# Scores of 13 chunks laid across all partitions through a line of DRAM instead of a TensorE transpose, and gate's row spread one turn earlier

## The chip, the cores and the metric

The kernel runs on one core of one Trainium2 chip. The metric is device time in microseconds: 203.6 us before the change, the median of three runs (203.56 to 203.7). The profile is of one execution, with a span of 201.8 us from first to last instruction.

## The reference

Two blocks follow one another. The first is a linear attention with data-dependent decay (RWKV6): for each batch and head a state of 48 x 48 is carried over 768 time steps.

```python
for t in range(S):
    cur = np.einsum('bhd,bhe->bhde', u[None] * kt, vt)
    y[:, :, t] = np.einsum('bhd,bhde->bhe', rt, state + cur)
    state = wt[:, :, :, None] * state + np.einsum('bhd,bhe->bhde', kt, vt)
```

Here (batch, heads, steps, head size) is (4, 8, 768, 48). The result, as x of (4, 768, 384), goes into a mixture of depths: a row's score is its product with w_gate; in each batch the 128 rows with the highest scores pass through a two-layer network, are weighted and added back.

```python
scores = np.einsum('bsd,d->bs', x, w_gate)
top_idx = np.argpartition(-scores[b], capacity)[:capacity]
ye = np.maximum(x[b, top_idx] @ w1, 0.0) @ w2
out[b, top_idx] = x[b, top_idx] + sigmoid(scores[b, top_idx])[:, None] * ye
```

All is in float32. The last line is shortened here; the reference writes the sigmoid out.

## The kernel before

The 768 steps of a batch are cut into NCH = 6 chunks of L = 128, which makes 24 chunks over B = 4 batches, numbered through: chunks 0 to 5 are batch 0, chunks 6 to 11 batch 1, and so on. The function `turn(i)` writes the work of one turn, from -2 to 24. The order is written out by hand (`tc.manual_schedule`): each engine runs its instructions in exactly the order in which `turn` names them, and the framework only adds the waits. A turn mixes work on several chunks, called by `step(function, chunk)`:

- `scores` (L379) for chunk i: the products of K and R into ps_s; `masked` (L387) on VectorE makes sc from it; `back` (L272, L397) turns K round again; `outputs_t` (L412 with sc, L420 with the carried state) makes ps_yt, which ScalarE copies into yt (L425).
- for chunk i-1: `rows_out` turns yt into rows (ps_y, L272), ScalarE copies them (L436), GpSimd adds the own term (L437), and SyncE sends x to out (L438). `row_products` (L442, GpSimd) and `row_sums` (L447, ScalarE) make the chunk's 128 scores, a column of `score` with one value in each partition.
- for chunk i+1: `inputs_t` transposes r (L265, ps_t), and `scaled` (L343) makes R from it with the scan `left`; for K likewise with the scan `right`.
- for chunk i+2: `decays_t` transposes w (L265, ps_w), and `scans` (L285, L291, L293, L296) runs the two running products on VectorE.
- `loads(i+5)`: SyncE issues v, k, r and w some turns ahead; `load_weights` sends a piece of w1 or w2 in seven of the turns.

What the change touches is `compared`. To find a row's rank, each score of a batch must be compared with every other. One of two must then stand along the free dimension, equal in all partitions. For chunk i-2, TensorE transposes the score column, repeated to 128 x 128, into ps_e (L508); VectorE compares the chunk's own scores with those of the earlier chunks (L510, on `every`) and with its own chunk (L514, on ps_e); ScalarE copies ps_e into `every` for the chunks to come (L519). ps_e and ps_w share the pool psW, which has one buffer: ps_w must wait until ps_e has been read, and ps_e until the scans have read the last ps_w. `compared` stands ahead of `masked` in the turn.

After the last chunk of a batch, `mixture` counts the lost comparisons on TensorE (ps_r, L534), picks the 128 rows (L551, ps_i L558), gathers them by an indirect transfer (L573) and transposes them (L582). Their two layers (`forward`: ps_h L618, ps_f L630) are fed in pieces into the turns of the next batch; those of the last batch come at the end. `spread(wg_bc, wg_row)` puts the row of w_gate in all partitions with two matmuls (ps_b, L258) and a ScalarE copy (L259); it stands in turn 0, behind `back`. `warm` is a filler matmul on zeros (ps_n, L253).

Of the kernel before, what the change touches and what calls it, by code (L numbers as in the profile page):

```python
# [10 lines left out]
FP32 = mybir.dt.float32  # L11
# [7 lines left out]
L = 128  # L19
# [6 lines left out]
def _rows(ap, n):  # L26

    return dataclasses.replace(ap, ap=[[0, n]] + [list(x) for x in ap.ap])
# [10 lines left out]
def kernel(  # L39
# [40 lines left out]
    nc = tc.nc  # L80
    PSUM = bass.MemoryType.PSUM

    B, H, S, D = r.shape
# [3 lines left out]
    NCH = S // L  # L87
# [11 lines left out]
    setup = ctx.enter_context(tc.tile_pool(name="setup", bufs=1))  # L99
    lev = ctx.enter_context(tc.tile_pool(name="lev", bufs=2))  # L100
    mod = ctx.enter_context(tc.tile_pool(name="mod", bufs=1))
    psW = ctx.enter_context(tc.tile_pool(name="psW", bufs=1, space=PSUM))
    psT = ctx.enter_context(tc.tile_pool(name="psT", bufs=2, space=PSUM))
    psS = ctx.enter_context(tc.tile_pool(name="psS", bufs=1, space=PSUM))
# [4 lines left out]
    chunks = [(b, ci) for b in range(B) for ci in range(NCH)]  # L109
# [17 lines left out]
    for queue, hs in ((nc.sync, slice(H // 2, H)), (nc.scalar, slice(0, H // 2))):  # L127
        queue.dma_start(
            out=w_bufs[0][:, hs, 0:D], in_=w[0, hs, 0:L, :].rearrange("h t d -> t h d")
# [4 lines left out]
    wg_row = setup.tile([1, C], FP32)  # L134
    nc.scalar.dma_start(out=wg_row, in_=_rows(moe_w_gate, 1))
    u_bc = consts.tile([L, H, D], FP32)
    wg_bc = consts.tile([L, C], FP32)
# [46 lines left out]
    ident = consts.tile([L, L], FP32)  # L184
# [13 lines left out]
    for x in (0, 1):  # L198
        for to, src in ((0, DP * x), (D, DP * (1 - x)), (2 * D, D)):
            n = min(D, DE - to)  # L200
# [12 lines left out]
    for t, sign in ((before_f, 1), (after_f, -1)):  # L213
        nc.gpsimd.memset(t, 1.0)
        nc.gpsimd.affine_select(
            out=t, in_=t, pattern=[[sign, L]], base=-1, channel_multiplier=-sign,
# [28 lines left out]
    score = consts.tile([L, B, NCH], FP32)  # L245
# [3 lines left out]
    def warm(n):  # L249

        ps = psM.tile([L, 512], FP32, tag="m", name="ps_n")
        for _ in range(n):
            nc.tensor.matmul(ps, nothing[:, 0:L], nothing, start=True, stop=True)  # L253

    def spread(to, row):

        ps = psM.tile([L, C], FP32, tag="m", name="ps_b")
        nc.tensor.matmul(ps, one_row, row, start=True, stop=True)  # L258
        nc.scalar.copy(out=to, in_=ps)  # L259
# [229 lines left out]

    against = {}  # L490

    def compared(t):

        b, ci = chunks[t["n"]]
        if ci == 0:
            while len(against) > 1:
                mix()
            against[b] = (
                mod.tile([L, S - L], FP32, name="every", bufs=2),
                mod.tile([L, NCH, S], BF16, name="ahead", bufs=2),  # L500
                lost_bufs[b % 2],
            )
        every, ahead, lost = against[b]
        own = score[:, b, ci:ci + 1]
        lo, hi = ci * L, (ci + 1) * L

        ps = psW.tile([L, L], FP32, tag="w", name="ps_e")
        nc.tensor.transpose(ps, own.to_broadcast([L, L]), ident)  # L508
        if ci > 0:
            nc.vector.tensor_scalar(  # L510
                out=ahead[:, ci, 0:lo], in0=every[:, 0:lo], scalar1=own, scalar2=None,
                op0=ALU.is_ge, op1=ALU.add, accum_out=lost[:, ci, 0:1],
            )
        nc.vector.scalar_tensor_tensor(  # L514
            out=ahead[:, ci, lo:hi], in0=ps, scalar=own, in1=after_f,
            op0=ALU.is_ge, op1=ALU.mult, accum_out=lost[:, ci, 1:2],
        )
        if ci < NCH - 1:
            nc.scalar.copy(out=every[:, lo:hi], in_=ps)  # L519

    def mixture(b):
# [130 lines left out]
    def step(f, n, *more):  # L652
        if 0 <= n < N:
            f(work.setdefault(n, dict(n=n)), *more)

    def mix(n=1, place=None):


        while n > 0 and mixing:
            if place is not None and mixing[0][1] not in (None, place):  # L660
                return
            try:
                mixing[0][1] = next(mixing[0][0])
                n -= 1
            except StopIteration:
                mixing.pop(0)
# [16 lines left out]
    def fed_in_turn(n, few):  # L683

        kept = (feed or picked) and (feed or picked)[0][0] == B - 2
        fed(few if kept else n, on=False)
# [6 lines left out]
    def turn(i):  # L693
        soon = i >= N - 1
        step(first_left, i + 1)
        if i < 1:
            step(scaled_aside, i + 1, "K", "right")
        step(own_products, i + 1)
        step(scores, i)
        step(own_values, i)  # L700
        step(carry, i - 1, work.get(i))
        if i > 0:
            step(scaled, i + 1, "K", "right")
        if i >= 0:
            step(own_weights, i + 1)
        if soon:
            step(masked, i)
        if i == N - 1:
            sums.extend(check_sums())
        if i < N:  # L710
            step(compared, i - 2)
        if not soon:
            step(masked, i)
        step(back, i)
        if i == 0:
            spread(wg_bc, wg_row)
        mix(place="half")
        step(rows_out, i - 1, soon)
        step(row_scores_soon if soon else row_products, i - 1)
        step(own_results, i)  # L720
        fed_in_turn(PIECES // 2, 2 if i >= N - 1 else 1)
        step(inputs_t, i + 1, "R", r_bufs)
        if i == -1:
            warm(1)
        step(scaled, i + 1, "R", "left")
        step(decays_t, i + 2)
        mix(place="mid")
        if i == -2:
            warm(2)
        step(range_check, i + 2)  # L730
        if i == -1:
            spread(u_bc.rearrange("p h d -> p (h d)"), u_row)
            step(own_weights, i + 1)
        step(outputs_t, i)
        step(carry_products, i)
        fed_in_turn(PIECES - PIECES // 2, 1 if i == N - 1 else 0)
        if i == N - 1:
            step(compared, i - 1)
        step(inputs_t, i + 2, "K", k_bufs)
        if i == -2:  # L740
            warm(1)
        if not soon:
            step(row_sums, i - 1)
        step(scans, i + 2)
        if 0 <= i - 2 < N - 1 and chunks[i - 2][1] == NCH - 1:
            mixing.append([mixture(chunks[i - 2][0]), "end"])
        mix(place="end")
        if i > -2:
            loads(i + 5)
        if i in WEIGHT_TURNS:  # L750
            load_weights(1)
# [23 lines left out]
    def general(gen):  # L775
        u_t = gen.tile([D, H], FP32, name="u_t")
        nc.sync.dma_start(out=u_t, in_=u.rearrange("h d -> d h"))
        for b in range(B):
            st = gen.tile([D, H, D], FP32, name="st")
            nc.vector.memset(st, 0.0)  # L780
            with tc.For_i(0, S) as i:
                now = {}
                for name, x in (("r", r), ("k", k), ("w", w)):
                    now[name] = gen.tile([D, H], FP32, name=f"{name}_t")
                    src = x[b, :, bass.ds(i, 1), :].rearrange("h o d -> d (h o)")
                    nc.sync.dma_start(out=now[name], in_=src)
                v_t = gen.tile([D, H, D], FP32, name="v_t")
                src = v[b, :, bass.ds(i, 1), :].rearrange("h o d -> (h o) d")
                nc.sync.dma_start(out=v_t, in_=_rows(src, D))
                kv = gen.tile([D, H, D], FP32, name="kv")  # L790
                nc.vector.tensor_mul(kv, v_t, now["k"].to_broadcast([D, H, D]))
                cur = gen.tile([D, H, D], FP32, name="cur")
                nc.vector.tensor_mul(cur, kv, u_t.to_broadcast([D, H, D]))
                nc.vector.tensor_add(cur, cur, st)
                nc.vector.tensor_mul(cur, cur, now["r"].to_broadcast([D, H, D]))
                nc.vector.tensor_mul(st, st, now["w"].to_broadcast([D, H, D]))
                nc.vector.tensor_add(st, st, kv)
                ps = psM.tile([L, C], FP32, tag="m", name="ps_g")
                nc.tensor.matmul(
                    ps[0:1], ones_f[0:D], cur.rearrange("p h d -> p (h d)"),  # L800
                    start=True, stop=True,
                )
                y_t = gen.tile([1, C], FP32, name="y_t")
                nc.scalar.copy(out=y_t, in_=ps[0:1])
                nc.sync.dma_start(out=out[b, bass.ds(i, 1), :], in_=y_t)
            for c in range(NCH):
                x = lev.tile([L, C], FP32, tag="x", name="x", bufs=3)
                nc.sync.dma_start(out=x, in_=out[b, c * L:(c + 1) * L, :])
                t = dict(n=b * NCH + c, x=x)
                row_scores_soon(t)  # L810
                compared(t)
            for _ in mixture(b):
                pass
            fed(1000)

    with tc.If(outside > 0):
        with tc.tile_pool(name="gen", bufs=1) as gen:
            general(gen)
# [26 lines left out]
```

## Time and profile before

| What | Value |
|---|---|
| Time, median of 3 | 203.6 us |
| Span of the profile | 201.8 us |
| TensorE matmul busy | 189.9 us (94%) |
| VectorE busy | 161.2 us (80%) |
| GpSimd busy | 136.7 us (68%) |
| ScalarE busy | 121.0 us (60%) |
| ps_e transposes (L508) | 24, 7.6 us, 318 ns each |
| Compare with earlier chunks (L510) | 20, 12.1 us, 605 ns each |
| Compare with own chunk (L514) | 24, 8.4 us, 348 ns each |
| Copy of ps_e into every (L519) | 20, 5.3 us, 263 ns each |
| Packets of SyncE's queue | 104304, 75.1% of 16 DMA engines' span |

Busy time is a sum over an engine's records; on TensorE records overlap, since matmuls are pipelined. The chain of work that ended last is followed back from the last instruction: at each step to what released it, or to the instruction before it on its engine. In order of time it lists start, length and what; "issue" is time in which the profile shows no reason to wait. In the timeline a note in brackets gives the idle time before an instruction and what ended it. SPq is SyncE's queue: there an instruction's length is that of the issue[...]. The DMA engines are at least nine tenths busy in nearly all of the first 100 us.

### The profile page before, as it was taken

How to read it: one execution, taken by the hardware profiler on the slowest of the kernel's cores; microseconds unless marked ns; L12 is line 12 of the kernel's file. 1: busy time of each engine (PE TensorE's matmuls, PEld its weight loads, DVE VectorE, ACT ScalarE, POOL GpSimd, SP SyncE). 2: the span in 40 equal slices, each digit the busy share in tenths (PEclk: the TensorE clock that was granted, in tenths of full speed). 3: DMA queues.
4: the chain of work that ended last, by engine and by line, in shares of the span. 5: the costliest groups of instructions: out<-in, count | busy, mean ns of one | idle time of the engine just before them, and what ended most of it. 6: DMA issues, size and time to landing. Idle time of an engine off the chain costs nothing.

```text
span 201.8 us, 6402 instructions
## 1 busy us (share of the span) xinstructions
PE 189.9 (94%) x2290; PEld 153.6 (76%) x2290; DVE 161.2 (80%) x355; ACT 121.0 (60%) x620; POOL 136.7 (68%) x175
## 2 busy tenths in 40 slices
PE   7899999989799899999999999999999999999980
PEld 3478888768687688888887888898887888876940
DVE  6989999999999968988979788988979784961010
ACT  4486877768854775878354865878354866510300
POOL 8497889886857996678538898669538898111202
PEclk9999999999999999999999999999999999999998
DMA  7999999999999999999892994998772221111101
GB/s 115 164 163 153 175 191 206 247 205 216 203 158 255 234 172 217 225 236 180 146 157 59 176 189 105 147 165 151 125 117 68 49 81 44 39 42 42 39 8 44
DMA packets 105387, 28.81 MB, mean 143 GB/s; under 512 B 100482, under 2 KB 104580, under 8 KB 105348
## 3 DMA queue, kind: packets, MB, share of 16 engines
q1 hardware_dynamic: 104304, 26.65, 75.1%
q0 software_dynamic: 512, 1.57, 2.6%
q8 instruction: 20, 0.33, 0.7%
q14 instruction: 19, 0.16, 0.3%
q10 hardware_dynamic: 532, 0.10, 0.3%
HBM read 22.81 MB, written 5.51 MB: 140 GB/s over the span
## 4 chain that ended last, share of the span: by engine, by line
PE 86%; DVE 5%; ACT 2%; POOL 2%; issue 2%; POOLq 0%; DVEq 0%; ACTq 0%
PE ps_s L379 12%; PE ps_h L618 11%; PE ps_f L630 11%; PE ps_yt L412 11%; PE ps_t L265 9%; PE ps_w L265 6%; PE ps_yt L420 5%; PE ps_kv L467 5%; PE ps_y L272 4%; PE ps_t L272 4%; PE ps_e L508 3%; PE ps_n L253 1%; DVE left L296 1%; DVE right_buf L285 1%; PE ps_r L534 1%
## 5 line engine op out<-in xcount | busy, mean ns | idle before, releaser
L364 ACT ACTIVATE rk<-rk 128x48 f32<-128x48 f32 x192 | 43.7, 231 | 0.1
L364 ACT ACTIVATION_READ_ACCUMULATOR rk<-rk 128x1 f32 x192 | 36.3, 189 | 0.0
L437 POOL TENSOR_TENSOR x<-x,vo 128x384 f32<-128x384 f32 x22 | 22.1, 1005 | 19.9 <-ACT x L436 19.8
L425 ACT COPY yt<-ps_yt 128x512 f32<-128x512 f32 x24 | 14.1, 587 | 29.6 <-PE ps_yt L420 27.1
L296 DVE TENSOR_TENSOR_SCAN left<-ps_w,from_left 128x511 f32<-128x511 f32 x24 | 30.7, 1281 | 0.9
L285 DVE TENSOR_TENSOR_SCAN right_buf<-ps_w,from_right 128x511 f32<-128x511 f32 x24 | 29.1, 1211 | 1.1 <-PE ps_w L265 1.1
L387 DVE TENSOR_TENSOR sc<-ps_s,before_f 128x1024 f32<-128x1024 f32 x24 | 29.2, 1219 | 0.8 <-PE ps_s L379 0.8
L379 PE MATMUL ps_s<-R,K 48*128 48x128 f32 x384 | 27.9, 285 | 0.3 <-ACT yt L425 0.2
L412 PE MATMUL ps_yt<-sc,v_buf 128*64 128x128 f32 x384 | 26.3, 278 | 1.6 <-PE ps_w L265 1.4
L379 PEld LDWEIGHTS ps_s<-R,K 48*128 48x128 f32 x384 | 23.3, 187 | 3.9 <-issue 2.9
L618 PE MATMUL ps_h<-xeT,w 128*128 128x128 f32 x192 | 25.6, 280 | 0.2 <-ACT hid L623 0.2
L355 POOL TENSOR_TENSOR rk<-r_buf,k_buf 128x384 f32<-128x384 f32 x24 | 24.2, 1007 | 1.7 <-DMA r_buf<-in_r_dram 1.7
L412 PEld LDWEIGHTS ps_yt<-sc,v_buf 128*64 128x64 f32 x384 | 20.7, 136 | 6.0 <-PE ps_w L265 2.8
L358 POOL TENSOR_TENSOR rk<-rk,u_bc 128x384 f32<-128x384 f32 x24 | 24.1, 1003 | 1.1 <-DVE alls L291 0.5
L618 PEld LDWEIGHTS ps_h<-xeT,w 128*128 128x128 f32 x192 | 22.9, 192 | 1.6 <-ACT xeT L584 0.5
L630 PE MATMUL ps_f<-w,hid 128*128 128x384 f32 x64 | 23.8, 500 | 0.0
L442 POOL TENSOR_TENSOR scr<-x,wg_bc 128x384 f32<-128x384 f32 x22 | 22.0, 1000 | 1.7
L370 POOL TENSOR_TENSOR vo<-v_buf,own 128x384 f32<-128x384 f32 x24 | 19.9, 830 | 1.3 <-ACT rk L364 1.3
L343 DVE TENSOR_TENSOR R<-ps_t,left 128x512 f32<-128x512 f32 x24 | 16.4, 685 | 3.7 <-ACT own L596 1.3
L343 DVE TENSOR_TENSOR K<-ps_t,right_buf 128x512 f32<-128x512 f32 x22 | 15.1, 684 | 4.7 <-PE ps_t L265 4.7
L265 PE MATMUL ps_w<-ident,w_buf 128*128 128x128 f32 x96 | 15.4, 284 | 1.8 <-ACT every L519 1.0
L332 ACT ACTIVATE junk<-w_buf,high 128x384 f32<-128x384 f32 x24 | 15.0, 623 | 0.6 <-DMA w_buf<-in_w_dram 0.6
(112 smaller groups left out, 343.6 us busy)
## 6 DMA issues: line engine op xcount, KB each, us to landing
k_buf<-in_k_dram SPq DMA_DIRECT2D x24, 192.0 KB, 4.5
r_buf<-in_r_dram SPq DMA_DIRECT2D x24, 192.0 KB, 5.4
v_buf<-in_v_dram SPq DMA_DIRECT2D x24, 192.0 KB, 4.7
out_dram<-x SPq DMA_DIRECT2D x24, 192.0 KB, 3.0
w_buf<-in_w_dram SPq DMA_DIRECT2D x23, 192.0 KB, 4.5
w<-in_moe_w_dram SPq DMA_DIRECT2D x3, 512.0 KB, 5.7
w<-in_moe_w_dram SPq DMA_DIRECT2D x4, 384.0 KB, 4.9
w_buf<-in_w_dram ACTq DMA_DIRECT2D x1, 96.0 KB, 3.2
```

The source lines that it names most:

```text
L265: nc.tensor.transpose(ps[:, j, :], src(j), ident)
L285: nc.vector.tensor_tensor_scan(out=flat[:, W - 2::-1], data0=wt[:, W - 1:0:-1], data1=from_right.rearrange("p j t -> p (j t)")[:, W - 2::- ...
L296: nc.vector.tensor_tensor_scan(out=left.rearrange("p j t -> p (j t)")[:, 1:W], data0=wt[:, 0:W - 1], data1=start.rearrange("p j t -> p (j ...
L343: nc.vector.tensor_mul(out, t.pop(name + "t"), t.pop(by))
L355: nc.gpsimd.tensor_mul(rk, r_bufs[n % NBUF][:, :, 0:D], k_bufs[n % NBUF][:, :, 0:D])
L358: nc.gpsimd.tensor_mul(t["rk"], t["rk"], u_bc)
L364: nc.scalar.activation(out=rk[:, h, :], in_=rk[:, h, :], func=AF.Copy, accum_out=o[:, h:h + 1])
L379: nc.tensor.matmul(ps[:, q, j, :], t["K"][rows, j, :], t["R"][rows, j, :], start=True, stop=True,)
L387: nc.vector.tensor_mul(t["sc"].rearrange("p q j t -> p (q j) t"), ps.rearrange("p q j t -> p (q j) t"), _heads(before_f, 2 * HP),)
L412: nc.tensor.matmul(ps[half(c), j % 2, j // 2, :], vt[:, 2 * j + q, :], t["sc"][:, q, j, :], start=(j < 2), stop=(old is None), skip_group_ ...
L618: nc.tensor.matmul(ps[:, q, :], w1[:, dc, (f0 + q) * L:(f0 + q + 1) * L], xeT[:, dc, :], start=(dc == 0), stop=(dc == NDC - 1),)
L630: nc.tensor.matmul(ps, hid[:, fc, :], w2[:, fc, :], start=(fc == 0), stop=(fc == NFC - 1))
```

## The change

For 13 chunks (chunks 0 to 4 of batches 1 and 2, chunks 0 to 2 of batch 3; numbers 6 to 10, 12 to 16, 18 to 20) TensorE no longer transposes the scores and ScalarE no longer copies them. Instead SyncE writes the column of 128 scores as a line of 512 bytes into DRAM, at the end of the turn that made it (`scores_out`), and in the next turn, behind the rows of the next chunk, reads that line back into all 128 partitions of `every` (`scores_in`). VectorE compares one turn later than before, and at another place: behind R and ahead of the scans. Both comparisons then read `every` in SBUF. The other 11 chunks are compared as before. Besides, w_gate's row is spread in turn -1, behind the transposes of the first r, in place of one filler. The aim is to take work from TensorE and ScalarE, and to free psW of ps_e.

```diff
+    lines = ctx.enter_context(tc.tile_pool(name="lines", bufs=4, space=bass.MemoryType.DRAM))
...
+    def by_way_of_dram(n):
+        b, ci = chunks[n]
+        return 0 < b < B - 1 and ci < NCH - 1 or 0 < b == B - 1 and ci < NCH - 3
+
+    def scores_out(t):
+        n = t["n"]
+        if by_way_of_dram(n):
+            b, ci = chunks[n]
+            t["line"] = lines.tile([1, L], FP32, name="line")
+            nc.sync.dma_start(
+                out=t["line"].rearrange("o (p q) -> (o p) q", q=1), in_=score[:, b, ci:ci + 1]
+            )
+
+    def scores_in(t):
+        n = t["n"]
+        if by_way_of_dram(n):
+            b, ci = chunks[n]
+            every = table(b)[0]
+            nc.sync.dma_start(
+                out=every[:, ci * L:(ci + 1) * L],
+                in_=_rows(t.pop("line").rearrange("o p -> (o p)"), L),
+            )
+
-    def compared(t):
+    def compared(t, late=False):
+        if late != by_way_of_dram(t["n"]):
+            return
...
-        ps = psW.tile([L, L], FP32, tag="w", name="ps_e")
-        nc.tensor.transpose(ps, own.to_broadcast([L, L]), ident)
+        if late:
+            ps = every[:, lo:hi]
+        else:
+            ps = psW.tile([L, L], FP32, tag="w", name="ps_e")
+            nc.tensor.transpose(ps, own.to_broadcast([L, L]), ident)
...
-        if ci < NCH - 1:
+        if not late and ci < NCH - 1:
             nc.scalar.copy(out=every[:, lo:hi], in_=ps)
...
-        if i == 0:
-            spread(wg_bc, wg_row)
         mix(place="half")
         step(rows_out, i - 1, soon)
         step(row_scores_soon if soon else row_products, i - 1)
+        step(scores_in, i - 2)
         step(own_results, i)
...
         if i == -1:
-            warm(1)
+            spread(wg_bc, wg_row)
         step(scaled, i + 1, "R", "left")
+        step(compared, i - 3, True)
         step(decays_t, i + 2)
...
         mix(place="end")
+        step(scores_out, i - 1)
         if i > -2:
             loads(i + 5)
```

More of the change, by code (lines that the diff above doesn't have):

```diff
@@ L490, with table @@
     against = {}
-    def compared(t):
-        b, ci = chunks[t["n"]]
-        if ci == 0:
+    def table(b):
+        if b not in against:
             while len(against) > 1:
@@ L502, in compared @@
             )
-        every, ahead, lost = against[b]
+        return against[b]
+    def by_way_of_dram(n):
[21 more added lines that the diff above has]
+            return
+        b, ci = chunks[t["n"]]
+        every, ahead, lost = table(b)
         own = score[:, b, ci:ci + 1]
         lo, hi = ci * L, (ci + 1) * L
-        ps = psW.tile([L, L], FP32, tag="w", name="ps_e")
-        nc.tensor.transpose(ps, own.to_broadcast([L, L]), ident)
+        if late:
[3 more added lines that the diff above has]
+            nc.tensor.transpose(ps, own.to_broadcast([L, L]), ident)
         if ci > 0:
@@ L810, in general @@
                 row_scores_soon(t)
-                compared(t)
+                scores_out(t)
+                scores_in(t)
+                compared(t, by_way_of_dram(t["n"]))
             for _ in mixture(b):
```

## The prediction

> **What bounds the kernel now.** I read the busy shares first, then the chain of work that ended last, then the same chain in order of time, then the timeline of single turns. A turn is one chunk of 128 rows; I number turns as the code does, by the chunk whose scores ps_s (L379) are computed in it.
>
> ```profile
> PE 189.9 (94%) x2290; PEld 153.6 (76%) x2290; DVE 161.2 (80%) x355; ACT 121.0 (60%) x620; POOL 136.7 (68%) x175
> PE 86%; DVE 5%; ACT 2%; POOL 2%; issue 2%; POOLq 0%; DVEq 0%; ACTq 0%
> out_dram<-x SPq DMA_DIRECT2D x24, 192.0 KB, 3.0
> ```
>
> TensorE (PE) is busy 94% of the span and carries 86% of the chain, so work taken from TensorE counts. How much one score transpose (ps_e, L508) counts is read from two neighbouring turns in the chain (start, length, what): turn 1 has no ps_e, turn 2 has one.
>
> ```profile
> 15.66 1.09 PE ps_s L379 x16
> 16.76 0.53 PE ps_t L272 x4
> 17.29 0.38 PE ps_y L272 x4
> 17.67 0.64 PE ps_t L265 x4
> ...
> 21.65 1.09 PE ps_s L379 x16
> 22.75 0.25 PE ps_e L508
> 23.00 0.38 PE ps_t L272 x4
> 23.38 0.38 PE ps_y L272 x4
> 23.77 0.33 PE ps_t L265 x3
> ```
>
> The group says 318 ns for one ps_e and the chain 0.25 us. But from the end of ps_s to R's transposes it is 17.67 - 16.76 = 0.91 us without ps_e and 23.77 - 22.75 = 1.02 us with it. The other 0.14 us is the turn-around after ps_s, which ps_t then pays (0.53 instead of 0.38). One ps_e costs 0.11 us.
>
> The turn where ps_e costs more is turn 9, after the first gather:
>
> ```profile
> 67.71 1.22 DVE L387 TENSOR_TENSOR sc<-ps_s,before_f 128x1024 f32<-128x1024 f32 x1
> 68.70 2.12 SPq L148 DMA_DIRECT2D r_buf<-in_r_dram  x1
> 68.82 0.24 ACT L519 COPY every<-ps_e 128x128 f32<-128x128 f32 x1
> 68.85 0.68 DVE L343 TENSOR_TENSOR R<-ps_t,left 128x512 f32<-128x512 f32 x1
> 69.12 0.66 PE L265 MATMUL ps_w<-ident,w_buf 128*128 128x128 f32 x4 [0.52 <-ACT every L519]
> ```
>
> ps_w and ps_e share the single buffer of psW, so ps_w waits until ScalarE has copied ps_e into every, and that copy stands in line behind eight rk sums. SyncE's r_buf issue takes 2.12 us here against 0.6 to 0.8 us in later turns: the queue is full in this stage, and SyncE goes from one transfer to the next without a gap.
>
> **What the Trainium skill says.** (1) "TensorE: Matmul & The Clock Gate", Part 4: PE-mode transpose, gives about 275 ns for a 128x128 transpose inside a kernel; records here agree (272 to 323 ns), but the two turns above show 0.11 us of added time, and I use that. (2) Its table before the first section says that ScalarE and VectorE queues are strictly first in, first out; the copy behind the rk sums agrees. (3) "DMA: Bandwidth & Descriptors", Rules for kernel authors: a transfer that reads what another wrote must wait for the other's semaphore, and a last dimension that is not contiguous becomes one descriptor per element. So each score column goes out as 128 pieces of 4 bytes, and the reading transfer waits on SyncE. (4) Same page, Latency and other measured facts: a round trip to HBM takes at least about 0.8 us. No transfer of the profile before is this small; its own row transfers (out_dram<-x) land after 2.0 to 5.5 us, and these I use.
>
> **The change part by part.**
>
> *Gate's row.* Today two ps_b matmuls of turn 0 take 0.84 us of the chain (at 11.69). They move to turn -1, in place of one filler (ps_n), where TensorE waits for the left scan anyway (ps_w at 7.99 has an idle time of 0.54 us before it). In turn 0, R's transposes would start at 11.69, but VectorE still makes sc until 12.8, so R moves from 13.21 to 12.8: 0.4 us. Bounds: 0 (the early loads set the pace; one rk product waits 0.97 us for r_buf at 16.24) to 0.7 (ps_yt, held only by sc: 13.55 to 12.85). Taken: -0.4.
>
> *Thirteen transposes.* 13 x 0.11 = 1.4 us. Bounds: 13 x 0.11 to 13 x 0.25 = 3.25. Taken: -1.4.
>
> *Thirteen ScalarE copies.* 13 x 0.26 us leave ScalarE, which is 60% busy; this counts only where ps_w waits for them. Turn 9: ps_s ends at 66.65; plus 0.91 gives R's transposes at 67.56; plus 0.44 (them), 0.44 (ps_w) and 0.33 (ps_x) puts ps_yt at 68.8, and sc, begun at 67.0 when K is done, is ready by 68.2. It starts at 70.10 today: -1.3. In turns 11 and 17 the chain shows ps_w at 0.60 instead of 0.44 us: -0.3. Sum -1.6; bounds -0.8 to -1.9.
>
> *The compare, a turn later.* VectorE's work stays the same (0.35 us for the own block and 0.35 to 0.87 us for the earlier ones); it moves from ahead of sc to between R and the scans. A turn with the longest compare fills some 6.6 us of VectorE's time (from start to start: K 0.61, compare 1.07, sc 1.14, R 0.61, scans and what is between 2.85, mid 0.27) against about 7.05 us that the turn takes. A turn that compares two chunks (13 and 19) is followed by a VectorE idle time of 1.41 us before rank (103.89), which hides the second. Reading SBUF instead of PSUM I take as free of charge. Cost 0.
>
> *The line of DRAM.* 26 transfers, about 0.4 us of SyncE each. Loads have room: k of chunk 12, issued at 67.66, is first transposed at 81.0, so these do not suffer. The risk is the new wait: the late compare waits on VectorE for every, and behind it stand both scans, then K and sc of the next turn. Line in is issued after the previous chunk's rows, about 3.7 us into a turn; the compare comes at about 3.9 us of the next, so there are 6.8 us for issue and landing. From turn 13 on, rows land after 2.0 to 4.4 us: in time. In batch 1 the queue is full and SyncE is late. Chunk 6: rows_out at 66.67, plus 0.4 (the line out before it) and 0.45, plus a landing of 4.4 gives 71.9, while R is done at about 68.8: a wait of 3 us. Chunk 9: rows_out at 86.00, plus four turns at 0.45 (an estimate between 0, since SyncE only waits for room there, and 0.8, two issues), plus 0.45 and 4.5 gives 92.8; compare 0.7, scans 2.85, mid and K 0.88, sc 1.14 end at 98.4, and ps_yt(13) could begin 0.8 us before its 99.22. Without the wait it would be 1.3 + 5 x 0.11 + 0.16 = 2.0 us earlier. So the wait gives back +1.2; bounds 0 (SyncE's extra issues hidden, landing nearer 2 us) and +3.2 (landing 2 us longer, as 4-byte pieces may).
>
> *Chunk 20.* Its late compare (0.35 + 0.27 us) lands in turn 23, between row_scores (L455, ends 174.6) and the compare of chunk 22 (174.75), where VectorE leads to x, score, rank and the last gather with almost no gap:
>
> ```profile
> 174.05 0.56 DVE L455 CUSTOM_DVE_ANT_0 scr<-x,wg_bc 128x384 f32<-128x384 f32 x1
> 174.53 0.08 DVE L455 DVE_READ_ACCUMULATOR2_ANT score<- 128x1 f32 x1
> 174.75 0.75 DVE L510 TENSOR_SCALAR_CACHE_REDUCE ahead<-every,score 128x512 bf16<-128x512 f32 x1
> 175.92 0.56 DVE L434 TENSOR_TENSOR x<-ps_y,vo 128x384 f32<-128x384 f32 x1
> ```
>
> Each line begins as the one before ends. Taken +0.5; bounds 0 to 0.6.
>
> Sum: -0.4 - 1.4 - 1.6 + 1.2 + 0.5 = -1.7, so 203.6 - 1.7 = 201.9.
>
> **The rivals.** *The line is always in time*: no give-back, -2.9, 200.7. For it: SyncE's long issues are waits for room, into which small issues fit. Against it: rows land 4.4 us after issue in batch 1. *The chain's price for ps_e holds*: 0.25 instead of 0.11 each, no waits: -0.4 - 3.25 - 1.6 + 0.5 = -4.75, 198.85. For it only that the chain states 0.25; turns 1 and 2 speak against it. *The line is late*: landing 2 us longer, give-back 3.2 and the start's 0.4 lost among the loads: -1.4 - 1.6 + 3.2 + 0.5 = +0.7, 204.3, slower than before. For it: 4-byte pieces into a full queue, and two waits on SyncE in line ahead of the loads. Against it: batches 2 and 3 have room of 2 us and more.
>
> **How the numbers follow.** Forecast 0.45, always in time 0.25, chain's price 0.10, late 0.20. The range takes in 200.7 and the late case's 204.3, and goes down to 199.2, short of the chain's price: 199.2 to 204.3. Faster by over 0.2% (below 203.2): the first three cases, less 0.04 for a forecast case with more give-back: 0.76. Within: these 0.04 and 0.04 of the late case, whose landing may be less than 2 us longer: 0.08. Slower: 0.16.
>
> **What would show it.** Right: 11 ps_e instead of 24; ps_t (L272) after ps_s at 0.53 in batches 1 and 2; no wait of ps_w for every in turns 8 to 20; idle time of VectorE put down to a DMA of every, nearly all between 68 and 95 us; ps_b off the chain after 10 us; the stretch from turn 14 to 20 shorter by less than 1 us. Wrong: VectorE waits for every after 100 us too (late case), no such wait at all (in time), or turns of batch 2 shorter by a quarter of a us each (chain's price). Also wrong if the loads now come late, seen as POOL or TensorE waiting for k_buf, r_buf or w_buf.

## The result, and the profile after

| | Before | After |
|---|---|---|
| Time, median (4 runs each) | 203.6 us | 277.6 us (273.3 to 280.4) |
| Ratio, 95% interval | 1 | 1.347 (1.339 to 1.354) |
| Span of the profile | 201.8 us | 273.4 us |

The change costs 74 us by the medians; 201.9 us had been forecast, with 204.3 us as the upper end. Two of the four runs after were disturbed, and ratios, here and below, leave such runs out: by the ratio the loss is 70.6 us.

From the page and the list of transfers of the changed kernel: busy time, TensorE's busy tenths and its granted clock in 40 slices, the chain that ended last, and three rows of transfers with the median time from issue to landing in us at the end. Such a median covers only the transfers whose landing the trace gives.

```profile
PE 208.7 (76%) x2276; PEld 167.7 (61%) x2276; DVE 162.1 (59%) x355; ACT 119.3 (44%) x607; POOL 136.9 (50%) x175
PE   7999998899198593284998849939179887939990
PEclk9999999999689959586899968968959999868998
PE 18%; DMA 12%; SPq 2%; DVE 2%; ACT 2%; another core or an unknown queue 2%; issue 1%; POOL 1%; POOLq 0%; DVEq 0%; ACTq 0%
out_dram<-x SPq DMA_DIRECT2D x24, 192.0 KB, 9.1
line<-score SPq DMA_DIRECT2D x13, 0.5 KB, 10.2
xe<-out_dram,idx POOLq DMA_INDIRECT x4, 9.1
```

TensorE had 94% of the span and now has 76%, though it has 14 instructions fewer: it waits, most slices with a gap show a lower granted clock (0.885 on average, 0.996 before), and its busy time is longer (208.7 us, 189.9 before). The chain can be followed back only to 160.8 us; in that part DMA has 12% of the span and TensorE 18%. The rows of x (out_dram) were not changed, and yet they land late: the trace gives the landing of only two of them, 6.0 and 12.2 us after the issue; before, those known took 1.8 to 4.5. Nor were the four gathers (xe), which GpSimd issues on a queue of its own. Three of them, each issued 3 to 6 us behind a line, land after 11.6, 8.2 and 9.9 us, the last, with no line under way, after 3.2; before it was 5.5, 3.5, 3.1 and 3.2. So what holds transfers up is not confined to SyncE's queue.

Who waits for it is in the list of waits (us in all, times, longest):

```profile
DVE ahead L547 <- DMA every<-line: 56.0, 9, 13.8
DVE ahead L543 <- DMA every<-line: 15.1, 3, 8.2
```

L547 is the comparison that the change made late; L543, the comparison with earlier chunks, is in these three cases one that stayed early. SyncE's issues around the first line, chunk 6 (start, length of the issue, what):

```profile
59.51 0.38 SPq L514 DMA_DIRECT2D line<-score  x1
59.98 0.42 SPq L149 DMA_DIRECT2D v_buf<-in_v_dram  x1
60.49 0.81 SPq L149 DMA_DIRECT2D k_buf<-in_k_dram  x1
61.39 2.57 SPq L149 DMA_DIRECT2D r_buf<-in_r_dram  x1
64.06 7.02 SPq L149 DMA_DIRECT2D w_buf<-in_w_dram  x1
71.13 2.94 SPq L181 DMA_DIRECT2D w<-in_moe_w_dram  x1
74.16 0.42 SPq L439 DMA_DIRECT2D out_dram<-x  x1
74.67 0.38 SPq L523 DMA_DIRECT2D every<-line  x1
```

The line is issued at once. Behind three more transfers the issue of w takes 7.02 us (0.6 to 2.1 us for the issues of w from 60 us on before the change). I read this as a queue without room; the trace does not show the queue itself. So the rows of chunk 7 and the read of the line, which stand behind it in program order, leave SyncE some 7 us late. VectorE, which has finished R, waits for that read, and with it everything behind on its engine:

```profile
67.75 0.68 DVE L344 TENSOR_TENSOR R<-ps_t,left 128x512 f32<-128x512 f32 x1
80.16 0.35 DVE L547 SCALAR_TENSOR_TENSOR ahead<-every,score,after_f 128x128 bf16<-128x128 f32 x1 [11.73 <-DMA every<-line]
```

How long one line takes shows near the end, where no load is left to compete. The chain in order of time:

```profile
229.00 8.64 DMA line<-score
237.64 0.02 issue
237.66 0.02 SPq L523
237.67 0.03 issue
237.70 4.10 DMA every<-line
```

512 bytes, cut into 128 pieces of 4, take 8.64 us from issue to landing; reading them back into 128 partitions (64 KB) takes 4.10 us. The trace gives the landing of six other lines: 8.4 to 11.7 us, median 10.2.

### The profile page after: what moved, and what is told of

It is laid out like the page before. It is cut to its first block, busy times and chain, and to the rows that moved or that the text cites. A ratio compares the mean times of both kernels' runs of the same rounds, so it can differ in the third digit from the quotient of the medians.

```text
span 273.4 us, 6374 instructions
## 1 busy us (share of the span) xinstructions
PE 208.7 (76%) x2276; PEld 167.7 (61%) x2276; DVE 162.1 (59%) x355; ACT 119.3 (44%) x607; POOL 136.9 (50%) x175
## 3 DMA queue, kind: packets, MB, share of 16 engines
q0 software_dynamic: 512, 1.57, 2.3%
## 5 line engine op out<-in xcount | busy, mean ns | idle before, releaser
L547 DVE SCALAR_TENSOR_TENSOR ahead<-every,score,after_f 128x128 bf16<-128x128 f32 x13 | 6.0, 458 | 60.7 <-DMA every<-line 56.0
L413 PE MATMUL ps_yt<-sc,v_buf 128*64 128x128 f32 x384 | 32.3, 320 | 3.9 <-DVE sc L388 2.3
L266 PE MATMUL ps_t<-ident,r_buf 128*128 128x128 f32 x96 | 16.6, 301 | 21.4 <-DVE K L344 21.3
L651 PE MATMUL ps_h<-xeT,w 128*128 128x128 f32 x192 | 28.5, 302 | 4.9 <-ACT hid L656 4.9
L413 PEld LDWEIGHTS ps_yt<-sc,v_buf 128*64 128x64 f32 x384 | 25.6, 161 | 9.5 <-DVE sc L388 3.8
L484 POOL TENSOR_TENSOR state<-mid,alls 128x192 f32<-128x192 f32 x16 | 8.2, 509 | 45.8 <-DVE mid L483 28.0
L651 PEld LDWEIGHTS ps_h<-xeT,w 128*128 128x128 f32 x192 | 25.8, 212 | 6.5 <-ACT hid L656 5.2
L266 PEld LDWEIGHTS ps_t<-ident,r_buf 128*128 128x128 f32 x96 | 12.2, 154 | 24.4 <-DVE K L344 22.2
L266 PE MATMUL ps_w<-ident,w_buf 128*128 128x128 f32 x96 | 17.6, 314 | 10.5 <-DVE ahead L547 8.3
L305 ACT COPY left<-from_left 128x1 f32<-128x1 f32 x24 | 4.4, 185 | 43.5 <-DVE from_left L294 40.1
```

Of the source, the lines that this page charges most:

```text
L266: nc.tensor.transpose(ps[:, j, :], src(j), ident)
L413: nc.tensor.matmul(ps[half(c), j % 2, j // 2, :], vt[:, 2 * j + q, :], t["sc"][:, q, j, :], start=(j < 2), stop=(old is None), skip_group_ ...
L651: nc.tensor.matmul(ps[:, q, :], w1[:, dc, (f0 + q) * L:(f0 + q + 1) * L], xeT[:, dc, :], start=(dc == 0), stop=(dc == NDC - 1),)
```

## The experiments

Three theories stood after the result. *Queue*: the pieces themselves are slow in DRAM and hold back what stands behind them, read or not. *Wait*: VectorE's wait for the line is the loss, and more distance would cure it. *Rest*: even a fast line would not have brought what was forecast. Each time below stands beside the kernel before on the same chip, 203.56 to 203.64 us.

**Written, and read by nobody (1).** The kernel before, plus the 13 writes of the change; no one waits for them.

```diff
+            nc.sync.dma_start(
+                out=t["line"].rearrange("o (p q) -> (o p) q", q=1), in_=score[:, b, ci:ci + 1])
...
+        step(scores_out, i - 1)
```

> The kernel before (TensorE transposes, early compare) with the 13 columns of scores also written as lines into DRAM; nobody reads the lines. Theory A (the writes of 4-byte pieces block the queue behind them): most of the 74 us are here, 255 to 277 us, SyncE's w_buf issues of 5 us and more. Rival B (the new waits of VectorE and SyncE on a round trip are what costs): no more than 1 us over 203.6, since nothing waits for the line.

247.0 us, ratio 1.213 (1.201 to 1.226): +43.4 us with no reader at all, though less than the 255 us and more that the theory expected. SyncE's issue of w behind the line at 95.65, and one wait:

```profile
99.05 8.05 SPq L149 DMA_DIRECT2D w_buf<-in_w_dram  x1
```

```profile
POOL rk L356 <- DMA r_buf<-in_r_dram: 30.9, 9, 7.3
```

GpSimd waits 30.9 us for r, against 1.7 us before: the loads come late. The first three gathers on GpSimd's own queue land late here too, after 9.6 to 13.0 us. The writes alone thus make more than half of the loss. Whether a line issued by another engine than SyncE would spare the loads was not tried; the late gathers speak against it.

**The same pieces 2 KB apart (2), and into one row of SBUF (3).** Only the destination differs:

```diff
+            t["line"] = lines.tile([L, 512], FP32, name="line")          # (2)
+            nc.sync.dma_start(out=t["line"][:, 0:1], in_=score[:, b, ci:ci + 1])
...
+            t["line"] = mod.tile([1, L], FP32, name="line", bufs=4)      # (3)
+            nc.sync.dma_start(out=t["line"], in_=score[:, b, ci:ci + 1])
```

> As the run before, but each 4-byte piece goes to its own row of 2 KB in DRAM instead of 128 neighbours in 512 bytes. Theory A1 (neighbouring pieces are written one after another, about 54 ns each): back to about 204 us, landing 2 to 3 us. Theory A2 (each 4-byte write to DRAM takes its DMA engine some 0.9 us, eight in a row): as slow as the run before, landing about 9 us.

> As the first run, but the 128 pieces of 4 bytes go to one row of SBUF instead of DRAM. Theory A (DRAM writes below some size are what is slow): about 204 us, landing about 2 us. If any 4-byte piece is slow wherever it goes: as slow as the first run.

203.59 us, ratio 1.0003 (0.9993 to 1.0013), and 203.57 us, ratio 0.9998 (0.9988 to 1.0008). Neither costs anything; the column lands after a median of 2.5 us both times (11 of 13 landings known). Kernel (2), the first line and the issue of w behind it:

```profile
59.57 0.38 SPq L503 DMA_DIRECT2D line<-score  x1
...
64.17 0.77 SPq L149 DMA_DIRECT2D w_buf<-in_w_dram  x1
```

As many pieces of 4 bytes from the same 128 partitions (SyncE's queue has 106176 packets in (1) and in (2)), and the issue takes 0.77 us instead of 7.02. So it is neither the number of pieces nor their size, but where in DRAM they fall.

**64 bytes apart (4) and 8 bytes apart (5).** As (2), with shorter rows:

```diff
-            t["line"] = lines.tile([L, 512], FP32, name="line")
+            t["line"] = lines.tile([L, 16], FP32, name="line")           # (4)
+            t["line"] = lines.tile([L, 2], FP32, name="line")            # (5)
```

> The kernel before with the 4-byte pieces of the score columns written to DRAM 64 bytes apart instead of side by side; nobody reads them. If only pieces within one 64-byte block wait for each other: about 203.6 us, as with 2 KB. If the block is larger (512 bytes): eight pieces for each block and a loss of some 1 to 5 us; if all within one page of several KB queue up, as slow as side by side, 247 us.

> The kernel before with thirteen unread columns written as 4-byte pieces 8 bytes apart, so that 8 instead of 16 pieces lie in each 64 bytes of DRAM. If pieces within one 64-byte block are written one after another, the line lands after about half the extra time (2.5 + 0.5 x 7 = 6 us) and the kernel loses about half of 43 us or less, 215 to 227 us. If only pieces that touch one another are slow, it is 203.6 us.

(4): 203.63 us, ratio 1.0006 (0.9997 to 1.0015), free again; three landings are known, 4.1, 4.5 and 1.4 us. (5): 211.2 us, ratio 1.037 (1.035 to 1.039). Its row of transfers:

```profile
line<-score SPq DMA_DIRECT2D x13, 0.5 KB, 6.3
```

The landing of 6.3 us is the 6 us expected; the time is not, 7.5 us lost instead of 11 to 23. If a block has 64 bytes, which these runs do not show by themselves, a piece has 15 neighbours in its block in the changed kernel, 7 in (5) and none in (2). What one neighbour costs in landing then comes out alike. For the first five lines, in a busy queue, the median landing is 3.8 us in (2), 6.4 in (5) and 10.3 in the changed kernel: (6.4 - 3.8) / 7 = 0.37 us and (10.3 - 3.8) / 15 = 0.43. For the last ones, in a nearly idle queue, it is 1.4 in (2), some 4.1 in (5) and 8.64 in the changed kernel: 0.39 and 0.48. What the landing costs the kernel is not in proportion; my guess is that most of the shorter one passes into the loads' slack.

**The reads alone (6).** 13 reads of a line of 512 bytes into 128 partitions, of data that is there from the start, used by nobody.

```diff
+            spare = mod.tile([L, L], FP32, name="spare", bufs=4)
+            nc.sync.dma_start(out=spare, in_=_rows(moe_w_gate[0:L], L))
...
+        step(scores_in, i - 2)
```

> The kernel before with only the 13 reads of a 512-byte line into all 128 partitions added, from w_gate into a tile that nobody uses. Theory A: within 0.7 us of 203.6. Rival C (128 readers of one line crowd one spot of DRAM): landing well over 5 us and 5 us or more in all.

203.58 us, ratio 1.0001 (0.9991 to 1.0011). The reading half, 13 x 64 KB, is free.

**Gate's row alone (7).** The kernel before with this move and nothing else.

```diff
-        if i == 0:
-            spread(wg_bc, wg_row)
...
         if i == -1:
-            warm(1)
+            spread(wg_bc, wg_row)
```

> Only gate's row moves from turn 0 to turn -1; all chunks are compared as before. The prediction's term: 0.4 us less (0 to 0.7), 203.2 us. Rival (early loads set the pace of the first turns): 203.6.

203.55 us, ratio 1.001 (0.999 to 1.003). No gain; the move belongs to no part of the loss either.

**The whole change with a fast line: turned (8), by way of a row (9).** In (8) VectorE turns the column in four blocks of 32 x 32, and the line is written as 4 pieces of 128 bytes. The write is also issued somewhat earlier, ahead of the turn's last piece of the mixture. In (9) the column goes into a row of SBUF, and this, behind the turn's loads, as one piece into DRAM: one transfer and one wait more.

```diff
+            four = mod.tile([L, 32], FP32, name="four", bufs=4)
+            nc.vector.transpose(out=four, in_=score[:, b, ci:ci + 1].to_broadcast([L, 32]))
-                out=t["line"].rearrange("o (p q) -> (o p) q", q=1), in_=score[:, b, ci:ci + 1]
+                out=t["line"].rearrange("o (q e) -> (o q) e", q=4), in_=four[0:L:32, :]
...
+            t["row"] = mod.tile([1, L], FP32, name="row_s", bufs=4)      # (9)
+            nc.sync.dma_start(out=t["row"], in_=score[:, b, ci:ci + 1])
+            nc.sync.dma_start(out=t["line"], in_=t.pop("row"))
```

> The changed kernel, but VectorE first turns the score column in its four blocks of 32 by 32, so that the line goes to DRAM in 4 pieces of 128 bytes instead of 128 pieces of 4. Theory A1 (only neighbouring small pieces were wrong, and the rest of the change does what the prediction said): about 201.9 us, 200.7 if the line is always in time; line lands in 2 to 4.5 us; hardly a wait for every after 100 us. Rival B (the round trip itself holds VectorE): above 210 us.

> The changed kernel, but the column goes as 4-byte pieces into one row of SBUF first and from there as one piece of 512 bytes into the line of DRAM, behind the loads of the turn; one transfer more per chunk, no work on VectorE. Theory A1: 202 to 203 us, a little over the run with VectorE's blocks, since a third landing of 2 to 4 us stands in the round trip. Rival B: above 210 us.

(8): 210.1 us, ratio 1.031 (1.027 to 1.035). (9): 217.5 us, ratio 1.066 (1.063 to 1.069); SyncE itself waits there, 2.7 us in all for the rows to land and 9.6 us for the lines, before it can issue the rest of its list. With the fast line of (8) all but 6.3 of the 70.6 us are gone, and the loads are in time (GpSimd waits 1.6 us for r). But the kernel is still slower than before, and not at the 200.7 us that a line in time was to give: for this rest the rival of the expectation, the round trip that holds VectorE, is the better one. The chain of (8):

```profile
93.67 0.68 SPq L439
...
94.44 4.26 DMA every<-line
...
98.82 0.23 DVE ahead L545
```

This is chunk 10's line, and its reader is the *early* compare of chunk 11, the last of its batch: it needs the scores of all earlier chunks and stands at the start of a turn, half a turn behind the issue of the read. 4.26 us do not fit, and VectorE stands 2.38 us before 98.82. Batch 2 has the same: a landing of 4.25 us and 1.57 us of standing before 145.61.

**Three tries at more distance, with an error of mine in each (10, 11, 12).** (10): the 4-byte line, ten chunks (without the last of the 13 in batches 1 and 2, one less in batch 3), compared two turns later than before instead of one. (That is one turn, some 7 us, more than in the change, and not the two turns and 14 us of the expectations below.) (11): the same with the turned line. (12): the turned line, eleven chunks, the change's own distance.

```diff
-        return 0 < b < B - 1 and ci < NCH - 1 or 0 < b == B - 1 and ci < NCH - 3
+        return 0 < b < B - 1 and ci < NCH - 2 or 0 < b == B - 1 and ci < NCH - 4    # (10), (11)
+        return 0 < b < B - 1 and ci < NCH - 2 or 0 < b == B - 1 and ci < NCH - 3    # (12)
...
-        step(compared, i - 3, True)
+        step(compared, i - 4, True)                                                 # (10), (11)
```

> The changed kernel with its line as 128 pieces of 4 bytes side by side, but for ten chunks instead of thirteen (the last two of batches 1 and 2 and the last four of batch 3, or as many as keep the late compare inside the loop, go to TensorE as before), and the compare two turns later than in the change, so that VectorE has some 14 us more before it needs the line. If the loss is VectorE's wait for the late line, the wait is gone and the time comes back to about 202 us. If the loss is the queue that the small pieces hold up, ten of thirteen holds remain: 203.6 + 10/13 x 43.4 = about 237 us, and VectorE's waits for every are near 0.

> The same ten chunks and the same two turns more, with the line written as 4 pieces of 128 bytes by the turned column. With neither the held queue nor the half-turn wait left, what the change takes from TensorE and ScalarE should show: 203.6 - 10 x 0.11 - 1.6 = about 200.9 us, and no wait for every over 0.5 us. If those savings lie off the path, as the gate's row did, it is 203.5 us.

> The turned line with the change's own distance of compare, but the chunk before the last of batches 1 and 2 (whose line is needed by the last chunk's early compare half a turn later) back on TensorE. If that half turn is what held the turned version at 210 us, two waits of about 2.5 to 4 us go, and the time is 202 to 204.5 us. If something else held it, it stays at 208 to 210 us.

(10): 261.9 us, ratio 1.282 (1.278 to 1.287). (11): 210.0 us, ratio 1.030 (1.026 to 1.034). (12): 208.9 us, ratio 1.028 (1.025 to 1.032). None tells what it was meant to: a chunk back on TensorE is compared early again, and that early compare now reads the line of the chunk before *it* half a turn after its issue. The wait had only moved from chunk 11 to chunk 10. In (11) VectorE stands 3.38 us before 92.17 and 2.72 us before 140.25, together 6.1 us, as much as the ratio says is lost; (13) shows that this agreement is partly luck. In (12) its waits for the line add up to 4.7 us of the 5.7 lost.

**The half turn really taken away (13 turned, 14 with 4 bytes).** As (11) and (10), but the first chunk after those with a line is transposed and copied early and compared a turn later.

```diff
+        if not late and kind(t["n"]) == 1:
+            nc.scalar.copy(out=every[:, lo:hi], in_=ps)
+            return
...
+        step(compared, i - 4, 2)
+        step(compared, i - 3, 1)
```

> The turned line for ten chunks, their compare at two turns more, and now also the first chunk after them in each batch: it is still transposed and copied early but compared a turn later, so that nothing reads a line sooner than a turn and a half after its write. If the half-turn wait, which the two runs before only moved to the chunk ahead, is what is left, it is gone: 203.6 us, or 201 us if the ten transposes and copies were on the path. If the line's other costs (26 issues on the queue, its waits for VectorE) hold it, it stays above 206 us.

> The same with the line as 128 pieces of 4 bytes. VectorE's waits for every should be near 0 and what is left is the held queue: 203.6 + 10/13 x 43.4 = about 237 us, against 261.9 us with the short waits and 203 us if the wait were the whole loss.

(14): 245.2 us, ratio 1.199 (1.194 to 1.205): 17 us less than (10), so the half-turn wait was that dear with the slow line, but in its profile (a run of 247.2 us) VectorE still waits 19.6 us for every, compared two turns late. Distance alone does not cure it. (13): 208.8 us, ratio 1.017 (1.014 to 1.020), with no wait for the line in its trace. Apart from VectorE's small turns of the column the two differ in the pieces alone: (1.199 - 1.017) x 203.6 / 10 lines = 3.7 us a line; in (1) it was 43.4 / 13 = 3.3. That is the price of the 4-byte pieces, in two different kernels, the first with a reader that waits. But (13) was not at 203.6: by the ratio it loses 3.4 us, only 2.7 less than (11). Something else was in it.

**What is left when the line is fast (15), and when there is no line (16, 17).** (15) is (13) with all late compares one turn later, as in the change. (16) is the changed kernel without any line: comparisons from batch 1 on use constant stand-ins for the scores, so it leaves out the order of the scores in these batches. (17) is (16) with ten chunks instead of thirteen, its compares placed as in (13).

```diff
-        step(compared, i - 4, 2)
+        step(compared, i - 3, 2)                                    # (15), against (13)
...
-        step(scores_in, i - 2)                                      # (16), against the change
-        step(scores_out, i - 1)
+        if b > 0 and made:
+            every, own = made[0], made[1][:, ci:ci + 1]
...
-        step(compared, i - 3, True)                                 # (17), against (16)
+        step(compared, i - 4, 2)
+        step(compared, i - 3, 1)
```

> The turned line for ten chunks as in the run before, with the chunk after them also compared late, but all late compares one turn later as in the change (not two), so that the last turn of a batch holds two compares on VectorE and not three. If VectorE's bunched compares ahead of the rank are what holds the run before at 208.8 us, about 2 x 1.5 us go: 203 to 206 us. If the line itself (its issues, SyncE's waits for the turned column) holds it, it stays at 206 to 209 us.

> The changed kernel without its line: neither the 13 writes nor the 13 reads. From batch 1 on the comparisons use constant stand-ins (tokens ranked by their place and not by their score), made once in turn 4, so that nothing is waited for; the 13 transposes on TensorE, the 13 copies by ScalarE and their waits are gone as in the change. So the order of the tokens in batches 1 to 3 is not that of the scores. It is the most that the change could have brought. By the prediction's terms (13 x 0.11 + 1.6) it is 203.6 - 3.0 = 200.6 us; if those terms lie off the path like the gate's row, 203.3 to 203.8 us.

> No line at all, with the constant stand-ins of the kernel without a line (tokens of batches 1 to 3 ranked by place, not by score), but its compares where the run of the turned line with two turns' distance has them: ten chunks two turns later and the next one turn later. If bunched compares on VectorE are the loss there, this kernel loses them too: 205.5 to 208 us against 202.8 us. If the line is the loss, it stays at 202.5 to 204 us.

(15): 204.5 us, ratio 1.008 (1.005 to 1.011). (16): 202.8 us (202.5 to 205.2), ratio 0.9991 (0.9965 to 1.0018). (17): 206.8 us, ratio 1.013 (1.010 to 1.016). Placing the compares as in (13) costs 1.9 us with a line ((13) against (15), by the ratios) and 2.8 us without one ((17) against (16), which differ in three chunks besides). In the profiled runs the spans differ by 3.9 and 4.1 us, but 1.2 us of the latter is there by turn 2 (sc at 24.40 in (17), 23.22 in (16)), ahead of any compare that was moved. So a loss of this size needs no line, and the place where it arises is VectorE: in both pairs the gap widens by 1.0 us from sc of turn 13 to sc of turn 14, at the end of batch 1. VectorE in (13), from R in the last turn of batch 1 to the first scan:

```profile
98.61 0.68 DVE L344 TENSOR_TENSOR R<-ps_t,left 128x512 f32<-128x512 f32 x1
99.20 0.60 DVE L555 TENSOR_SCALAR_CACHE_REDUCE ahead<-every,score 128x384 bf16<-128x384 f32 x1
99.73 0.90 DVE L559 SCALAR_TENSOR_TENSOR ahead<-every,score,after_f 128x128 bf16<-128x128 f32 x1
...
100.56 0.73 DVE L555 TENSOR_SCALAR_CACHE_REDUCE ahead<-every,score 128x512 bf16<-128x512 f32 x1
...
101.23 0.42 DVE L559 SCALAR_TENSOR_TENSOR ahead<-every,score,after_f 128x128 bf16<-128x128 f32 x1
...
101.58 1.21 DVE L286 TENSOR_TENSOR_SCAN right_buf<-ps_w,from_right 128x511 f32<-128x511 f32 x1
```

Two late compares fill 2.4 us between R and the scans, with no gap; ahead of them, in the same turn, is the early one of chunk 11. Behind the scans come rank and the picks, which the gather needs. In the kernel before that place held nothing. SyncE's waits for the turned column, 17 us in all in the profile of (15), cost little: (15) loses 1.6 us by its ratio, and everything else of the change is in that as well.

(16) is the ceiling of the change as its compares are placed: a line that costs nothing gains 0.1% by the ratio, 0.4% by the medians, and the interval includes no gain at all; it is not 3 us. Where that gain goes is seen in the start times of sc on VectorE, read from the timelines (us):

| Turn | 9 | 12 | 13 | 14 | 18 | 19 | 22 |
|---|---|---|---|---|---|---|---|
| Before | 67.71 | 90.16 | 97.28 | 106.21 | 135.28 | 142.40 | 166.17 |
| Without line (16) | 66.60 | 88.80 | 97.19 | 105.42 | 133.75 | 142.14 | 164.88 |
| Gained | 1.11 | 1.36 | 0.09 | 0.79 | 1.53 | 0.26 | 1.29 |

It builds up to 1.4 us by turn 12 and is given back in turn 13, the same in 18 and 19. (16), VectorE in that stretch:

```profile
91.49 0.60 DVE L538 TENSOR_SCALAR_CACHE_REDUCE ahead<-f,f 128x384 bf16<-128x384 f32 x1
92.02 0.08 DVE L538 DVE_READ_ACCUMULATOR ahead<-f,f 128x1 f32 x1
92.02 0.47 DVE L542 SCALAR_TENSOR_TENSOR ahead<-f,f,after_f 128x128 bf16<-128x128 f32 x1
...
95.53 0.68 DVE L343 TENSOR_TENSOR K<-ps_t,right_buf 128x512 f32<-128x512 f32 x1
96.12 0.87 DVE L538 TENSOR_SCALAR_CACHE_REDUCE ahead<-f,f 128x640 bf16<-128x640 f32 x1
96.92 0.08 DVE L538 DVE_READ_ACCUMULATOR ahead<-f,f 128x1 f32 x1
96.92 0.35 DVE L542 SCALAR_TENSOR_TENSOR ahead<-ps_e,f,after_f 128x128 bf16<-128x128 f32 x1
...
97.19 1.22 DVE L387 TENSOR_TENSOR sc<-ps_s,before_f 128x1024 f32<-128x1024 f32 x1
```

From 91.49 to 98.4 no idle time: chunk 9's late compare (0.93 us to 92.42) and chunk 11's early one (1.07 us) both lie between the sc of turn 12 and that of turn 13. Before, only one compare lay there. That the two compares use up the gain is read from this trace; no run has them elsewhere. No version beats the kernel before by more than its measurement can tell.

## Why the prediction was wrong

**The failed step is "The line of DRAM".** It put the give-back at +1.2 us, "bounds 0 (SyncE's extra issues hidden, landing nearer 2 us) and +3.2 (landing 2 us longer, as 4-byte pieces may)". Landing times were borrowed from out_dram, "2.0 to 5.5 us", whose pieces are long rows. (Even these were misread: the known landings of the rows are 1.8 to 4.5 us, and 3.2 at most from turn 13 on, where the prediction has 4.4; 5.5 us is the first gather.) A line of 4-byte pieces side by side took 8.4 to 11.7 us, and the whole line cost some 70 us. The upper bound was a row's landing and 2 us, and no bound.

**"Loads have room … so these do not suffer" was wrong too**, and is the larger half. The step asked whether loads come late by the two extra issues on SyncE (0.4 us each), not what a slow write does to the transfers behind it. Experiment (1) has the writes alone at +43.4 us, with 30.9 us of waits for r and 12.0 for k in its trace. The prediction did name the sign to look for (POOL or TensorE waiting for k, r or w); it gave that case no price.

**How the loss divides.** By the ratios it is 70.6 us. The writes alone make 43.4 of it (1). The other 27 or so appear only once VectorE waits for the late line (71 us of such waits in the trace, which overlap with what the writes hold up anyway). A fast line leaves 6.3 us (8), and 1.6 are left when the half turn is taken away as well (15, with ten lines and one more late compare in each batch). These parts were measured in different kernels, and their sum is not exact.

**The room of 6.8 us** was nearly right for the late compare with a fast line (1.7 us of waits in (8)) and left out a reader. The early compare of chunks 11 and 17 (and 21) also needs the line of the chunk before, with half that room: 15.1 us of waits in the changed kernel, 3.9 in (8), where they are the largest part of what is left.

**Gate's row, -0.4:** 0 (7). The lower bound was right, and for the reason it gave: with the row moved, R does start 0.4 us earlier, but the chain there runs through the load of k, which lands at 14.98, just ahead of K's transposes. **Transposes and copies, -1.4 and -1.6:** turn 9, most of the copies' term, was nearly right: it begins sc 1.11 us earlier in (16), against 1.3 forecast for ps_yt. The 0.11 us for each transpose were not measured alone. But of 3.0 us only 0.7 (medians) to 0.9 (spans, 201.8 and 200.9) reach the end. **"The compare, a turn later. Cost 0"** is why, as far as the trace of (16) tells. The step did see that VectorE fills 6.6 of 7.05 us of a turn, and that turns 13 and 19 hold two compares. But it looked for their cost behind the second, ahead of rank, and not at the late compare of the turn before and the early one, which both stand ahead of sc of turn 13 (and of 19); there 1.3 us are given back each time. A size was set to nothing, too: "Reading SBUF instead of PSUM I take as free of charge". The own-block compare takes 348 ns from PSUM and 516 ns from SBUF in (16), up to 1.03 us in single cases: 13 x 0.17 = 2.2 us more on VectorE, though only 0.13 of it in the stretch shown above. **Chunk 20, +0.5:** not seen; (16) is 0.87 us ahead when sc of turn 23 starts (170.39, before 171.26), ahead of that compare, and still 0.9 us ahead at the end.

**The rivals.** "The line is late" had the right sign and, in its arguments for, the right cause ("4-byte pieces into a full queue"), at 0.20 and a hundredth of the size: 0.7 us of loss for some 70. "Always in time" at 200.7 is 2.1 us below what even no line at all reaches with these compares (16); "the chain's price" is refuted by the same run.

## What to carry to other kernels

Before you send a column through DRAM, ask how its bytes lie at the destination: here 128 pieces of 4 bytes side by side took 8 to 12 us and made loads and gathers late, while the same pieces 64 bytes apart or into SBUF cost the kernel nothing, and turned first into 4 pieces of 128 bytes they left the loads in time. A landing time read from another shape of transfer bounds nothing. Here a transfer of 512 bytes was the slowest, and transfers behind it paid, on its own queue and on GpSimd's; so price the wait and the neighbours separately. When a value arrives later, list all its readers, and look which engine becomes full in the turn where the postponed work falls.

## What the runs showed of the hardware

The Trainium skill, "DMA: Bandwidth & Descriptors", Specifications, says that below 512 bytes, the least for full rate, the engines read, modify and write. What these runs show is not decided by that size: pieces of 4 bytes that are 64 bytes or more apart are as far below 512 and cost the kernel nothing ((2) and (4)), while 8 bytes apart they cost 7.5 us (5) and side by side 43.4 us (1). Reckoned by neighbours in 64 bytes, each adds 0.4 to 0.5 us to the landing. That neighbours are written one after another fits these numbers but was not seen directly; the step between 8 and 64 bytes was not divided further.

The compare from SBUF showed a second thing. All 24 own-block compares of the kernel before, with ps_e in PSUM, take 338 to 352 ns, also where a GpSimd instruction began before them and ended after them. Of the 13 in (16) with both block operands in SBUF, 12 begin under a GpSimd instruction, and each of these ends 0.14 to 0.17 us after it. In (16), GpSimd while VectorE's 0.76 us compare ran from 99.59 to 100.35:

```profile
99.37 0.83 POOL L370 TENSOR_TENSOR vo<-v_buf,own 128x384 f32<-128x384 f32 x1
```

99.37 + 0.83 = 100.20, and the compare ends 0.15 us later; at 68.33 one takes 1.03 us under a GpSimd product that ends at 69.21. The Trainium skill, "GPSIMD Engine Reference", 1. Specifications, says that GpSimd's way to SBUF is shared with VectorE and in contention with instructions that have two SBUF inputs; this trace agrees.
